# The last step of an inverse transform as three products over 128 rows, in place of four over 96

## The chip, the cores and the metric

One core of one Trainium2 chip. The metric is the device time of one execution, in microseconds.

## The reference

In short (the whole has intermediate names):

```python
def _attn_ref(x, filt_r, filt_i):           # x: 8 batches x 3008 tokens x 256 channels
    X = np.fft.rfft(x, axis=1)
    Y = X * (filt_r + 1j * filt_i)[None]
    return np.fft.irfft(Y, n=x.shape[1], axis=1).astype(np.float32)

def _moe_ref(x, w_gate, w_val, w_out):      # x: 24064 x 256, d_ff 1536
    g = x @ w_gate
    return (g / (1 + np.exp(-g)) * (x @ w_val) @ w_out).astype(np.float32)
```

Everything is fp32. Most of the time goes to the second part. The kernel does the transforms of batch b+1 between the products of batch b.

## The kernel before

A transform of 3008 = 47 x 64 tokens is done in steps. The change concerns the last step of the inverse one, `stage3`, and what feeds it. An intermediate `d2` in DRAM holds 48 rows (24 frequencies, real and imaginary) for each of 64 residues n2 and 256 channels. `load_t4` brings one piece of it, `stage3` multiplies by a table over the 96 rows (two halves h of 48), and ACT (ScalarE) and DVE (VectorE) evacuate the result, that is, bring it from PSUM to `y`. PE in the profile's lines is TensorE.

```python
def load_t4(self, k, i, part=None):
    # ... (the first chunk of batch 0 has a path of its own)
    t = t4pool.tile([NK, NH, C], FP32, ...)              # NK = 96, NH = 4, C = 256
    self.load(out=t, in_=self.d2_rows[:, ts(2 * k + i, NH), :])

def stage3(self, k, step):                               # step 0..3, k = chunk 0..3
    i, cb = divmod(step, 2)
    ps = ...                                             # one PSUM bank
    psv = ps...[:, 0:TH].rearrange("p (n r) -> p n r", n=NH)   # TH = 4 x 94 = 376
    for n in range(NH):
        pin(nc.tensor.matmul(out=psv[:, n, :], lhsT=self.t4[k, i][:, n, ts(cb, 128)],
                             rhs=wi_t, start=n == 0, stop=True, skip_group_check=True))
    yield
    # ... evacuations to y
```

In this text a block is one `stage3` step, with four products before and three after. A weight load brings `lhsT` into TensorE's array ahead of the matmul that uses it. A record is one entry of the profile's list of instructions. `pd` is the PSUM tile that a block writes, `wa`, `wk`, `we`, `wA`, `wF` and `wG` are tiles of the second part. Column 2 n1 + h of each 94 belongs to half h. So 94 columns of a product hold two interleaved sets of 47, each of which uses 48 of the 96 rows; the other half of the table is zeros. That is the waste that the change goes after.

Of the kernel before, what the change touches and what calls it, by code (L numbers as in the profile page):

```python
# [41 lines left out]
FP32 = mybir.dt.float32  # L42
U32 = mybir.dt.uint32
# [5 lines left out]
B, S, C = 8, 3008, 256  # L49
# [4 lines left out]
N1, N2 = 47, 64  # L54
NS, NQ = 24, 64
NR = 2 * N1
NK = 4 * NS

NH = 4
# [4 lines left out]
NT = 3  # L64
NG = 3
# [4 lines left out]
NV = 2  # L70
# [39 lines left out]
PIECES = ((0, 7), (7, 14), (14, 20), (20, 26))  # L110


def dft_tables():
    n1, n2 = np.arange(N1), np.arange(N2)
    s, q = np.arange(NS), np.arange(NQ)
    ph = 2 * np.pi * (np.outer(n1, s) % N1) / N1
    w = np.stack([np.cos(ph), -np.sin(ph)], 1)
    wf = np.zeros((N1, 2, NS, 2, 2))
    wi = np.zeros((NS, 2, 2, N1, 2))

    v = np.stack([2 * np.cos(ph), -2 * np.sin(ph)], 0)
    v[0, :, 0], v[1, :, 0] = 1.0, 0.0
    for h in range(2):
        wf[:, h, :, :, h] = w.transpose(0, 2, 1)
        wi[:, :, h, :, h] = v.transpose(2, 0, 1) / S


    kap = np.where(q[:, None] < 32, s + N1 * q[:, None], s + N1 * (95 - q[:, None]))
    sg = np.where(q < 32, 1.0, -1.0)[:, None]
    th = 2 * np.pi * ((n2[:, None, None] * kap) % S) / S  # L130
    c, sn = np.cos(th), np.sin(th)
    d = np.zeros((2, N2, NS, 2, NQ))
    d[0, :, :, 0] = c.transpose(0, 2, 1)
    d[1, :, :, 0] = sn.transpose(0, 2, 1)
    d[0, :, :, 1] = (-sn * sg).transpose(0, 2, 1)
    d[1, :, :, 1] = (c * sg).transpose(0, 2, 1)
    d = d.reshape(128, NS, 128)
    de = np.stack([d, d.transpose(2, 1, 0)], 2)
    f32 = np.float32
    return (wf.reshape(NR, NK).astype(f32), wi.reshape(NK, NR).astype(f32),  # L140
            np.ascontiguousarray(de).astype(f32))


@with_exitstack
def kernel(
# [8 lines left out]
    out: bass.AP,  # L154
):
    nc = tc.nc
    wf_host, wi_host, de_host = dft_tables()
    wf_dram = nc.inline_tensor(wf_host, name="wf_tbl")
    wi_dram = nc.inline_tensor(wi_host, name="wi_tbl")
    de_dram = nc.inline_tensor(de_host, name="de_tbl").ap()  # L160
    unit_dram = nc.inline_tensor(np.eye(128, dtype=np.float32), name="unit_tbl")

    def pool(name, bufs, space=None):
# [6 lines left out]
    t4pool = pool("t4", 2)  # L170
# [35 lines left out]
    one = cpool.tile([128, 1], FP32)  # L206
# [15 lines left out]
    pin = tc.keep_in_program_order  # L222

    def add(eng, dst, a, b):
        return eng.tensor_tensor(out=dst, in0=a, in1=b, op=ALU.add)  # L225
# [224 lines left out]
    preparation = Preparation()  # L450
    TICKS = 20



    def bank(name):
# [11 lines left out]
    class Spectral:  # L467


        def __init__(self, b):  # L470
            self.b = b
            self.d1, self.d2 = [dram_tiles[2 * (b % 2) + i] for i in range(2)]
            self.d1_rows = self.d1.rearrange("a (h n) c -> (a h) n c", h=2)
            self.d2_rows = self.d2.rearrange("a (h n) c -> (a h) n c", h=2)
            self.x, self.t2, self.f, self.tb, self.p, self.t4, self.y = {}, {}, {}, {}, {}, {}, {}
            self.real = {}
# [27 lines left out]
        def load_two(self, u):  # L504
            if u < N_TWO:
                self.tb[u] = lend("tb", u).rearrange("p i (k c) -> p i k c", k=2)
                self.load(out=self.tb[u], in_=de_dram[:, ts(u, NV)])

                f = lend("f", u).rearrange("p (k i) c -> p k i c", k=2)
                self.f[u] = f  # L510
                for rows, view in filter_parts():
                    r, part = rows.start, rows.start // 64
                    for at in (r, r + 64) if part == 0 else (r,):
                        self.load(out=f[at:at + 32, part], in_=view(NV * u, NV))
                self.t2[u] = lend("t2", u)
                self.load(out=self.t2[u], in_=self.twos(self.d1, u))
# [10 lines left out]
        def load_t4(self, k, i, part=None):  # L527
            if part is not None:

                t = f0[0:NK, ts(i, NH), :]  # L530
                r = (slice(0, 64), slice(64, NK))[part]
                self.load(out=t[r], in_=self.d2_rows[r, ts(i, NH), :])
            else:
                t = t4pool.tile([NK, NH, C], FP32, name=f"t4_{self.b}_{k}_{i}", tag="t4")
                self.load(out=t, in_=self.d2_rows[:, ts(2 * k + i, NH), :])
            self.t4[k, i] = t

        def bank(self, name):
# [76 lines left out]
        def stage2b(self, u):  # L615

            pt, tb = self.p.pop(u), self.tb.pop(u)
            ps = self.bank(f"pc_{self.b}_{u}")
            for i in range(NV):
                pin(nc.tensor.matmul(out=ps[:, i, :], lhsT=tb[:, i, 1, :],  # L620
                                     rhs=pt[:, i, :], start=True, stop=True))
            g = self.place("g", u)
            yield
            if self.b == 0 and u == N_TWO - 1:
                for i in range(NV):
                    pin(nc.scalar.copy(out=g[:, i], in_=ps[:, i]))
            else:
                pin(nc.scalar.copy(out=g, in_=ps))
            queue = nc.scalar if self.b or u >= 8 else nc.sync
            pin(queue.dma_start(out=self.twos(self.d2, u), in_=g))  # L630

        def stage3(self, k, step):

            if step == 0:
                self.y[k] = ypool.tile([128, 8, TQ], FP32, name=f"y_{self.b}_{k}", tag="y")
            i, cb = divmod(step, 2)
            ps = (self.bank if k == 0 else fbank)(f"pd_{self.b}_{k}_{step}")
            psv = ps.rearrange("p a b -> p (a b)")[:, 0:TH].rearrange("p (n r) -> p n r", n=NH)
            for n in range(NH):
                pin(nc.tensor.matmul(out=psv[:, n, :],  # L640
                                             lhsT=self.t4[k, i][:, n, ts(cb, 128)],
                                             rhs=wi_t, start=n == 0, stop=True,
                                             skip_group_check=True))
            yield

            y = self.y[k]

            def tokens(part, parts):
                return y[:, part:part + parts].rearrange("p t (r n) -> p n (t r)", n=NH)

            if cb == 0:
                pin(nc.scalar.copy(out=tokens(2 * i, 2), in_=psv))
                return
            for t in range(2):
                a, c = 2 * i + t, psv[:, :, ts(t, N1)]
                b, v, k = tokens(a, 1), tokens(4 + a, 1), KS[a]
                if k == 0:
                    pin(nc.scalar.copy(out=v, in_=c))
                elif k == -1:
                    pin(add(nc.vector, v, c, b))  # L660
                else:
                    pin(nc.vector.scalar_tensor_tensor(
                        out=v, in0=b, scalar=-float(k), in1=c, op0=ALU.mult, op1=ALU.add))
# [164 lines left out]
    rpool = pool("raw", 1)  # L828
# [11 lines left out]
    with tc.tile_pool(name="start", bufs=1) as spool0:  # L840
# [12 lines left out]
        n = 0  # L853
# [34 lines left out]
        for u in range(N_TWO + lag):  # L888
            if u < N_TWO:
                spec.turn(u + 2)  # L890
                step = spec.stage2a(u)
# [26 lines left out]
        for p in ("A13", "A01"):  # L918
            at = SLOT[p]
# [62 lines left out]
    def chore(step, token, f, *args):  # L982
        chores.setdefault((step, token), []).append((f, args))

    chore(0, "B01", lambda: combine_sequence(cur.y[0], 3))
    for step in range(NT):
# [3 lines left out]
        if step < NCHUNK - 2:  # L990
            for i in range(2):
                chore(step, "A23", lambda k, i: cur.load_t4(k, i), step + 2, i)
    chore(NT, "W2", keep_y, NT)
    for step in range(NT - 1, NT * NG):
        chore(step, "A02" if step < NT else "P0", lambda s: reload_y(order_of(0)[s + 1][0], s), step)
    for step in range(NT, NT * NG):
# [5 lines left out]
    for b in range(B):  # L1002
        cur, nxt = spec, following if b + 1 < B else None
# [7 lines left out]
        one = [nxt.stage1(u) for u in range(N_ONE)] if nxt else []  # L1011
        two = []
# [23 lines left out]
        for step in range(NCHUNK * NG + (b == B - 1)):  # L1036
            ghost = step == NCHUNK * NG
            k, g = order_of(b)[min(step, NCHUNK * NG - 1)]
            this = None
            pieces = []  # L1040
            if not ghost:
                pieces = plan[step]
                this = Group(b, k, g, cur.y[k], sequence_of(cur, nxt, step))
                if b == 0:
                    preparation.finish(step)
                chunk = {0: 1, 2: 2, 5: 3}.get(step)
                if b and chunk:
                    for i in range(2):
                        cur.load_t4(chunk, i)
            elif before is None:  # L1050
                break
            ends = {ORDER[e - 1]: n for n, (_, e) in enumerate(PIECES)}
            last = ghost or b == B - 1 and step == NCHUNK * NG - 1
            for place, token in enumerate(SCHEDULE):
# [4 lines left out]
                op = token.rstrip("'")  # L1059
                if op[0] == "t":  # L1060
                    n = int(op[1])
                    ps = pieces_before if old else pieces
# [15 lines left out]
                if b + 2 < B and (step, op) == (9, "B01"):  # L1078
                    for u in range(2):
                        following.load_x(u)  # L1080
                if nxt and (step, op) == (10, "A12" if b else "E23"):
                    for i in range(2):
                        nxt.load_t4(0, i)
                for f, args in chores.get((step, op), ()) if b == 0 else ():
                    f(*args)
# [36 lines left out]
```

## Time and profile before

| | before |
|---|---|
| median, first three runs | 2950.47 us |
| TensorE busy | 99% |
| blocks in all: 8 batches x 16 | 128, of which 112 change |

The profile's view of one tile, pd, in the kernel before: records with duration min/median/max in ns.

```profile
L640 PE MATMUL pd<-wi_t,t x992: 246/275/421, 78.5 to 2817.6; 96*128 96x94 f32 x199
L652 ACT COPY y<-pd x62: 833/843/871, 79.6 to 2811.9; 128x376 f32<-128x376 f32 x62
```

The first line counts eight records for a block of four products; the second is the evacuation that mustn't get dearer.

### The profile page before, as it was taken

The numbers are of one execution on the slowest core, as the hardware profiler recorded it, in microseconds if no ns is written. First come the engines' busy times: TensorE is split into PE (matmuls) and PEld (weight loads), VectorE is DVE, ScalarE is ACT, GpSimd is POOL, SyncE is SP. The second block draws the span as 40 slices with busy tenths as digits, with TensorE's granted clock in tenths as the row PEclk, the third lists the DMA queues.
The fourth block names the chain that finished last, engine by engine and source line by source line (L and its number), as shares of the span: only waits on it lengthen the run. The fifth ranks groups of instructions, "written<-read, shape, count | busy, mean of one in ns | idle before, by whom it ended". The sixth has DMA issues, their size and how long they took to land.

```text
span 2946.9 us, 57623 instructions
## 1 busy us (share of the span) xinstructions
PE 2911.7 (99%) x20264; PEld 2816.1 (96%) x20264; DVE 1929.3 (65%) x4384; ACT 1609.9 (55%) x4208; POOL 1579.8 (54%) x1759
## 2 busy tenths in 40 slices
PE   7999999999999999999999999999999999999999
PEld 5889999999999999999999999999999999999999
DVE  6888765576655676557765667656666566766666
ACT  6775455545555555555455554555555555555554
POOL 3876655556444655455554456454564545555453
PEclk9999999999999999999999999999999999999999
DMA  8677855575555655556646566556665565644442
GB/s 232 212 255 245 299 188 184 174 229 180 178 179 185 222 186 171 182 188 200 213 152 194 188 195 212 162 176 203 194 199 171 177 211 190 201 138 152 148 129 88
DMA packets 217452, 558.57 MB, mean 190 GB/s; under 512 B 29962, under 2 KB 107642, under 8 KB 217166
## 3 DMA queue, kind: packets, MB, share of 16 engines
q1 hardware_dynamic: 171326, 485.59, 51.5%
q10 hardware_dynamic: 36912, 45.43, 4.6%
q0 software_dynamic: 8928, 23.89, 2.3%
q8 instruction: 162, 2.65, 0.4%
q14 instruction: 124, 1.02, 0.1%
HBM read 459.73 MB, written 95.05 MB: 188 GB/s over the span
## 4 chain that ended last, share of the span: by engine, by line
PE 94%; DVE 1%; POOL 1%; DMA 1%; issue 0%; ACT 0%; SPq 0%; DVEq 0%; POOLq 0%
PE wa L732 24%; PE wA L811 17%; PE wk L732 16%; PE we L732 12%; PE wG L811 9%; PE wF L811 4%; PE pd L640 4%; PE pa L548 3%; PE pc L620 2%; PE pb L588 2%; DMA y_t<-yt 0%; POOL y_t L225 0%; DVE h L779 0%; POOL wt_t L225 0%; POOL wt_t L228 0%
## 5 line engine op out<-in xcount | busy, mean ns | idle before, releaser
L732 PE MATMUL wa<-y_t,wt_t 128*128 128x188 f32 x4464 | 880.2, 323 | 5.2 <-issue 1.4
L732 PEld LDWEIGHTS wa<-y_t,wt_t 128*128 128x128 f32 x4464 | 730.0, 190 | 30.1 <-issue 17.3
L225 POOL TENSOR_TENSOR h<-h 128x376 f32<-128x376 f32 x190 | 183.1, 985 | 787.1 <-DVE h L779 777.5
L811 PE MATMUL wA<-wo_t,h 128*128 128x128 f32 x4608 | 577.7, 275 | 2.5 <-DVE o L225 2.0
L811 PEld LDWEIGHTS wA<-wo_t,h 128*128 128x128 f32 x4608 | 562.9, 192 | 16.2 <-issue 10.4
L732 PE MATMUL wk<-y,wt_t 128*128 128x188 f32 x2976 | 567.9, 324 | 0.0
L228 POOL TENSOR_TENSOR h<-h 128x376 f32<-128x376 f32 x570 | 553.5, 993 | 0.5
L732 PEld LDWEIGHTS wk<-y,wt_t 128*128 128x128 f32 x2976 | 479.2, 191 | 25.9 <-issue 19.8
L228 DVE TENSOR_TENSOR we<-we,m 128x376 f32<-128x376 f32 x576 | 318.6, 556 | 196.9 <-PE we L732 138.4
L732 PE MATMUL we<-y_t,wt_t 128*128 128x188 f32 x2232 | 431.5, 323 | 1.4 <-ACT we L763 1.4
L732 PEld LDWEIGHTS we<-y_t,wt_t 128*128 128x128 f32 x2232 | 369.4, 190 | 1.8 <-ACT we L763 1.7
L228 POOL TENSOR_TENSOR D<-f,f 128x376 f32<-128x376 f32 x288 | 281.0, 989 | 104.6 <-ACT f L747 103.9
L232 DVE SCALAR_TENSOR_TENSOR y<-wk,c 128x376 f32<-128x376 f32 x480 | 245.1, 543 | 133.8 <-ACT we L763 83.2
L767 ACT COPY m<-wa 128x376 f32<-128x376 f32 x576 | 272.0, 472 | 88.2 <-PE wa L732 87.0
L774 ACT ACTIVATE g<-wa 128x188 f32<-128x188 f32 x576 | 188.1, 327 | 190.6 <-PE wa L732 182.6
L811 PE MATMUL wG<-wo_t,h 128*128 128x128 f32 x2304 | 288.3, 275 | 0.6 <-DVE o L225 0.6
L811 PEld LDWEIGHTS wG<-wo_t,h 128*128 128x128 f32 x2304 | 281.4, 192 | 0.8 <-DVE o L225 0.8
L774 ACT ACTIVATE u<-we 128x188 f32<-128x188 f32 x576 | 189.0, 328 | 168.8 <-DVE we L228 149.9
L747 ACT ACTIVATE f<-wk 128x376 f32<-128x376 f32 x288 | 139.3, 484 | 235.4 <-PE wk L732 214.3
L751 ACT COPY c<-wk 128x376 f32<-128x376 f32 x288 | 136.0, 472 | 226.0 <-PE wk L732 226.0
L754 DVE SCALAR_TENSOR_TENSOR x<-wk,f 128x376 f32<-128x376 f32 x192 | 104.6, 545 | 235.8 <-PE wk L732 230.0
L763 ACT COPY we<-y 128x376 f32<-128x376 f32 x480 | 224.1, 487 | 33.7 <-DVE h L779 14.7
(142 smaller groups left out, 3915.9 us busy)
## 6 DMA issues: line engine op xcount, KB each, us to landing
wt_t<-w_all SPq DMA_DIRECT2D x174, 896.0 KB
wt_t<-w_all SPq DMA_DIRECT2D x174, 768.0 KB
t<-d SPq DMA_DIRECT2D x62, 384.0 KB
d<-t ACTq DMA_DIRECT2D x112, 192.0 KB
lent<-de_tbl SPq DMA_DIRECT2D x84, 256.0 KB
lent<-in_filt_r_dram SPq DMA_DIRECT2D x336, 64.0 KB
lent<-d SPq DMA_DIRECT2D x84, 256.0 KB
d<-lent ACTq DMA_DIRECT2D x84, 256.0 KB
```

The source lines that it names most:

```text
L225: return eng.tensor_tensor(out=dst, in0=a, in1=b, op=ALU.add)
L228: return eng.tensor_tensor(out=dst, in0=a, in1=b, op=ALU.subtract)
L232: return nc.vector.scalar_tensor_tensor(out=dst, in0=a, scalar=-1.0, in1=b, op0=ALU.mult, op1=ALU.subtract)
L640: pin(nc.tensor.matmul(out=psv[:, n, :], lhsT=self.t4[k, i][:, n, ts(cb, 128)], rhs=wi_t, start=n == 0, stop=True, skip_group_check=True))
L732: pin(nc.tensor.matmul(out=ps[:, z], lhsT=self.wt[:, SLOT[p], z], rhs=rhs, start=start and z == 0, stop=True, skip_group_check=True))
L747: pin(act.mul(self.small(f"f{i}", f"f{i}", 1), t[f"k{i}"], -1.0))
L751: pin(act.copy(out=self.small(f"c{i}", f"c{i}", 1), in_=t[f"k{i}"]))
L754: pin(v.scalar_tensor_tensor(out=dst, in0=t[f"k{j}"], scalar=-1.0, in1=t[f"f{i}" if j == 3 else f"D{at}"], op0=ALU.mult, op1=ALU.add))
L763: pin(act.copy(out=self.bank(f"e{at}"), in_=t[f"y{at}"]))
L767: pin(act.copy(out=self.small(f"m{at}", "m", 4), in_=t[f"a{at}"]))
L774: pin(act.activation(out=self.small(op, "g", 3, 1)[:, 0], in_=ps[:, 1], func=AF.Silu))
L811: pin(nc.tensor.matmul(out=self.tiles[at][:, t, :], lhsT=self.hs[i][:, HID[p], t0:t0 + 128], rhs=wo_t[:, JB * q + i, WO[p], :], start=star ...
```

## The change

From batch 1 on, `d2` is kept by tokens with real and imaginary rows side by side. A group (n2, h) is then 48 adjoining rows, eight groups are 384 rows, and these fill three tiles of 128 rows without zeros. A group that lies across a tile's edge occurs in two products, so the products have 3, 4 and 3 groups of 47 columns: 141, 188 and 141.

```diff
+BACK = (((0, 0, 0, 48), (1, 48, 0, 48), (2, 96, 0, 32)),
+        ((4, 64, 0, 48), (5, 112, 0, 16), (2, 0, 32, 16), (3, 16, 0, 48)),
+        ((5, 0, 16, 32), (6, 32, 0, 48), (7, 80, 0, 48)))
 ... (tables: back from BACK; later = de with its columns in the new order)
-                self.load(out=self.tb[u], in_=de_dram[:, ts(u, NV)])
+                self.load(out=self.tb[u], in_=later_dram[:, ts(u, NV)])
 ... load_t4, from batch 1 on:
+                    rows = self.d2_tokens.rearrange("(h n) a c -> h (n a) c", h=2)
+                    rows = rows[:, ts(at, 2 * NS * NH)]
+                    for j in range(2):
+                        self.load(out=t[64 * j:64 * j + 64, 1],
+                                  in_=rows[j, 128 * (1 - j):128 * (1 - j) + 64])
+                        self.load(out=t[:, 2 * j], in_=rows[j, 64 * j:64 * j + 128])
 ... the store of d2, from batch 1 on:
+            rows = self.d2_tokens.rearrange("n (p s) c -> (n p) (s c)", p=2)
+            pin(queue.dma_start(out=rows[:, ts(u, NV * C)], in_=g.rearrange("q s c -> q (s c)")))
 ... stage3:
+            for j in range(len(BACK) if back else 0):
+                first = BACK_AT[j]
+                cols = back_t[0][:, first:first + N1 * len(BACK[j])]
+                if j == 1:
+                    rows = flat[:, 1:2 * 187 + 1].rearrange("p (z y) -> p z y", z=2)[:, :, ::2]
+                else:
+                    at = j // 2 * (2 * N1 + 1)
+                    rows = flat[:, at:at + 6 * N1 - 1:2]
+                pin(nc.tensor.matmul(out=rows, lhsT=self.t4[k, i][:, j, ts(cb, 128)], rhs=cols,
+                                     start=j == 0, stop=True, skip_group_check=True))
-            for n in range(NH):
+            for n in range(0 if back else NH):
 ... the second load of a chunk is issued later in its step; the table back is loaded once in batch 0
```

The order of columns in the bank is kept, so that evacuations stay as they are. Each product therefore writes every second element of the bank.

More of the change, by code (lines that the diff above doesn't have):

```diff
@@ L110 @@
 PIECES = ((0, 7), (7, 14), (14, 20), (20, 26))
+BACK = (((0, 0, 0, 48), (1, 48, 0, 48), (2, 96, 0, 32)),
+        ((4, 64, 0, 48), (5, 112, 0, 16), (2, 0, 32, 16), (3, 16, 0, 48)),
+        ((5, 0, 16, 32), (6, 32, 0, 48), (7, 80, 0, 48)))
+BACK_AT = (0, 3 * N1, 7 * N1)
 def dft_tables():
@@ L125, in dft_tables @@
         wi[:, :, h, :, h] = v.transpose(2, 0, 1) / S
+    one = wi[:, :, 0, :, 0].transpose(1, 0, 2).reshape(2 * NS, N1)
+    back = np.zeros((128, 10 * N1))
+    for tile_, first in zip(BACK, BACK_AT):
+        for i, (_, row, a, rows) in enumerate(tile_):
+            back[row:row + rows, first + N1 * i:first + N1 * (i + 1)] = one[a:a + rows]
     kap = np.where(q[:, None] < 32, s + N1 * q[:, None], s + N1 * (95 - q[:, None]))
@@ L138, in dft_tables @@
     de = np.stack([d, d.transpose(2, 1, 0)], 2)
+    pairs = np.arange(128).reshape(2, N2).T.ravel()
+    later = np.stack([de[:, :, 0], de[:, :, 1][:, :, pairs]], 2)
     f32 = np.float32
     return (wf.reshape(NR, NK).astype(f32), wi.reshape(NK, NR).astype(f32),
-            np.ascontiguousarray(de).astype(f32))
+            back.astype(f32), np.ascontiguousarray(de).astype(f32),
+            np.ascontiguousarray(later).astype(f32))
 @with_exitstack
@@ L156 @@
     nc = tc.nc
-    wf_host, wi_host, de_host = dft_tables()
+    wf_host, wi_host, back_host, de_host, later_host = dft_tables()
     wf_dram = nc.inline_tensor(wf_host, name="wf_tbl")
     wi_dram = nc.inline_tensor(wi_host, name="wi_tbl")
+    back_dram = nc.inline_tensor(back_host, name="back_tbl")
     de_dram = nc.inline_tensor(de_host, name="de_tbl").ap()
+    later_dram = nc.inline_tensor(later_host, name="later_tbl").ap()
     unit_dram = nc.inline_tensor(np.eye(128, dtype=np.float32), name="unit_tbl")
@@ L451, with load_back @@
     TICKS = 20
+    back_t = []
+    def load_back():
+        t = rpool.tile([128, 2, 128, 2], U32, name="back", tag="raw", bufs=2)
+        t = t.bitcast(FP32).rearrange("p b f two -> p (b f two)")
+        back_t.append(t[:, 0:10 * N1])
+        pin(nc.sync.dma_start(out=back_t[0], in_=back_dram.ap()))
     def bank(name):
@@ L473, in __init__ @@
             self.d1_rows = self.d1.rearrange("a (h n) c -> (a h) n c", h=2)
+            self.d2_tokens = self.d2.rearrange("a n c -> (a n) c").rearrange(
+                "(n a) c -> n a c", n=N2)
             self.d2_rows = self.d2.rearrange("a (h n) c -> (a h) n c", h=2)
@@ L533, in load_t4 @@
             else:
-                t = t4pool.tile([NK, NH, C], FP32, name=f"t4_{self.b}_{k}_{i}", tag="t4")
-                self.load(out=t, in_=self.d2_rows[:, ts(2 * k + i, NH), :])
+                t = t4pool.tile([128, NH, C], FP32, name=f"t4_{self.b}_{k}_{i}", tag="t4")
+                at = 2 * k + i
+                if self.b == 0:
+                    self.load(out=t[0:NK], in_=self.d2_rows[:, ts(at, NH), :])
+                else:
[5 more added lines that the diff above has]
+                        self.load(out=t[:, 2 * j], in_=rows[j, 64 * j:64 * j + 128])
             self.t4[k, i] = t
@@ L629, in stage2b @@
             queue = nc.scalar if self.b or u >= 8 else nc.sync
-            pin(queue.dma_start(out=self.twos(self.d2, u), in_=g))
+            if self.b == 0:
+                pin(queue.dma_start(out=self.twos(self.d2, u), in_=g))
+                return
+            rows = self.d2_tokens.rearrange("n (p s) c -> (n p) (s c)", p=2)
+            pin(queue.dma_start(out=rows[:, ts(u, NV * C)], in_=g.rearrange("q s c -> q (s c)")))
         def stage3(self, k, step):
@@ L638, in stage3 @@
             psv = ps.rearrange("p a b -> p (a b)")[:, 0:TH].rearrange("p (n r) -> p n r", n=NH)
-            for n in range(NH):
+            flat = ps.rearrange("p a b -> p (a b)")
+            back = self.b
+            for j in range(len(BACK) if back else 0):
[3 more added lines that the diff above has]
+                    rows = flat[:, 1:2 * 187 + 1].rearrange("p (z y) -> p z y", z=2)[:, :, ::2]
+                else:
+                    at = j // 2 * (2 * N1 + 1)
[3 more added lines that the diff above has]
+            for n in range(0 if back else NH):
                 pin(nc.tensor.matmul(out=psv[:, n, :],
-                                             lhsT=self.t4[k, i][:, n, ts(cb, 128)],
+                                             lhsT=self.t4[k, i][0:NK, n, ts(cb, 128)],
                                              rhs=wi_t, start=n == 0, stop=True,
@@ L993 @@
     chore(NT, "W2", keep_y, NT)
+    chore(NT * NG - 1, "P0", load_back)
     for step in range(NT - 1, NT * NG):
@@ L1047 @@
                 if b and chunk:
-                    for i in range(2):
-                        cur.load_t4(chunk, i)
+                    cur.load_t4(chunk, 0)
             elif before is None:
@@ L1080 @@
                         following.load_x(u)
-                if nxt and (step, op) == (10, "A12" if b else "E23"):
-                    for i in range(2):
+                if b and chunk and op == "B01":
+                    cur.load_t4(chunk, 1)
+                for i in range(2):
+                    if nxt and (step, op) == (10, ("A12", "E23")[i] if b else "E23"):
                         nxt.load_t4(0, i)
```

## The prediction

> **What bounds the kernel now.** I read first the page's shares and slices, then the chain that ended last, then TensorE's groups by shape, then TensorE's order of time in one stretch of a middle batch, and last the load queue's order of time in the same stretch.
>
> The page's first part and its slices:
> ```profile
> span 2946.9 us, 57623 instructions
> PE 2911.7 (99%) x20264; PEld 2816.1 (96%) x20264; DVE 1929.3 (65%) x4384; ACT 1609.9 (55%) x4208; POOL 1579.8 (54%) x1759
> PE   7999999999999999999999999999999999999999
> PEclk9999999999999999999999999999999999999999
> DMA  8677855575555655556646566556665565644442
> ```
> TensorE is busy from the second slice to the last at full clock. The other engines have a third or more of the span free and the DMA engines about two fifths. The page's chain says the same by line:
> ```profile
> PE 94%; DVE 1%; POOL 1%; DMA 1%; issue 0%; ACT 0%; SPq 0%; DVEq 0%; POOLq 0%
> PE wa L732 24%; PE wA L811 17%; PE wk L732 16%; PE we L732 12%; PE wG L811 9%; PE wF L811 4%; PE pd L640 4%; PE pa L548 3%; PE pc L620 2%; PE pb L588 2%; DMA y_t<-yt 0%; POOL y_t L225 0%; DVE h L779 0%; POOL wt_t L225 0%; POOL wt_t L228 0%
> ```
> So the end is set by the sum of TensorE's work, and what the change touches (tile pd, line 640) is 4% of it, some 105 to 130 us. TensorE's groups by shape (columns: line, engine, operation, out<-in, partitions x columns, count, then busy us and mean ns, then idle before):
> ```profile
> L732 PE MATMUL wa<-y_t,wt_t 128*128 128x188 f32 x4464 | 880.2, 323 | 5.2 <-issue 1.4 <-DMA y_t<-yt 1.3 <-ACT m L767 1.2
> L640 PE MATMUL pd<-wi_t,t 96*128 96x94 f32 x992 | 128.3, 272 | 0.0
> ```
> The pd products never waited for anything: idle 0.0. Their mean of 272 ns is a latency of overlapping instructions and not their price. The price is read from where one run of matmuls starts and the next starts. TensorE's order of time (start us, us, what):
> ```profile
> 1501.25 1.47 PE L732 MATMUL wk<-y,wt_t 128*128 128x188 f32 x8
> 1502.56 1.50 PE L811 MATMUL wA<-wo_t,h 128*128 128x128 f32 x12
> 1503.89 1.44 PE L732 MATMUL wk<-y,wt_t 128*128 128x188 f32 x8
> 1505.17 0.80 PE L732 MATMUL wa<-y_t,wt_t 128*128 128x188 f32 x4
> 1505.81 0.80 PE L732 MATMUL wk<-y,wt_t 128*128 128x188 f32 x4
> 1506.44 1.03 PE L640 MATMUL pd<-wi_t,t 96*128 96x94 f32 x8
> 1507.31 1.53 PE L811 MATMUL wA<-wo_t,h 128*128 128x128 f32 x12
> 1508.67 0.80 PE L732 MATMUL wk<-y,wt_t 128*128 128x188 f32 x4
> ```
> Each fp32 product of the program shows as two matmul records and two weight loads (8 records for a block of 4 products). A record with 188 columns takes (1505.81 - 1505.17)/4 = 160 ns, one with 128 columns (1503.89 - 1502.56)/12 = 111 ns, and one of pd with 94 columns (1507.31 - 1506.44)/8 = 109 ns. The last two are the point: 94 columns cost as much as 128. The pd products stand on a floor, and it isn't the streaming of columns.
>
> **What the Trainium skill says, and whether this trace agrees.** First, "TensorE: Matmul & The Clock Gate", section "LDWEIGHTS (loading the stationary operand)": a weight load takes the number of its columns divided by 1.2, in ns, whatever the contraction. For 128 columns that is 107 ns, and section "Back-to-back issue gap" gives a warm gap of N/2.4 + 2.5 ns. If each of the two records streams its columns at two cycles each (my reading), that is 2N/2.4 + 2.5: 159.2 ns for 188 (the trace has 160), 109 for 128 (111), 81 for 94. The trace has 109, so there the weight load binds. The page and the trace agree.
>
> Second, "PSUM — Partial Sum Buffer", section "Specifications (TRN2)": lines of 8 bytes, and "any non-contiguous AP slows matmuls significantly". The new products write every second fp32 element, one per 8-byte line. Every matmul of the kernel before writes adjoining columns, so its trace neither supports nor denies this. It is the main doubt.
>
> Third, "DMA: Bandwidth & Descriptors", section "Rules for kernel authors", on two transfers to disjoint partition halves: "Don't bother", as they share the same engines. The change splits one third of each load that way, so I expect no speed from it, only one more issue.
>
> **The change part by part.** The blocks: 8 batches x 4 chunks x 4 steps = 128 of 4 products, so 1024 records, which are the 992 above and 32 with another source tile. Batch 0 keeps its form, so 112 blocks change.
>
> Removed: 112 blocks of 8 records. The block above takes 870 ns; others of the same stretch took 860 (1500.39 to 1501.25), 870 and 860, so I use 865: 112 x 0.865 = 96.9 us.
>
> Added: 112 blocks of 3 products over 128 rows with 3, 4 and 3 groups of 47 columns, which is 141, 188 and 141. By the formula that the 188-column records confirm, a record of 141 columns takes 282/2.4 + 2.5 = 120 ns (an estimate from that page's section and this trace), just above the weight-load floor, and one of 188 takes 160. A block is 2 x (120 + 160 + 120) = 800 ns, and 112 x 0.800 = 89.6 us. The streamed columns rise from 376 to 470 a product set, but two of eight weight loads go. That is why the gain is so much less than the quarter that "three for four" suggests: 65 ns of 865, or 7.5%.
>
> The sum on TensorE: 96.9 - 89.6 = 7.3 us, 0.25% of the time. As TensorE is the bound and never waits, all of it should reach the end.
>
> Moved off the path: the evacuations to y (ACT and DVE) read the same PSUM layout, so they keep their durations. The store of d2 takes rows of 2 KB in place of 1 KB. A load of t4 takes four transfers with 384 rows of 1 KB in place of one with 96 rows of 4 KB; the bytes are the same. The issue records of SP show about 0.4 us for such a transfer, so a step with a chunk (two loads, one step of about 30 us in three) gets 6 x 0.4 = 2.4 us more on a queue that mostly waits for weight buffers. The load queue's order of time:
> ```profile
> 1487.86 0.80 SPq L479 DMA_DIRECT2D t<-d  x2
> 1488.76 38.34 SPq L376 DMA_DIRECT2D wt_t<-w_all  x7
> ```
> The two loads are issued by 1488.7, and the first block that reads them starts at 1500.39, 11.7 us later. The change also issues the second half of a chunk later in the step. By the program's schedule this one goes from 58% of a step to 82% of it, and its block comes at 47% of the next: 0.65 x 30 = 19 us. So there is room. The table is loaded once, in batch 0, into a buffer that the weights' preparation has left. The new transform table has the size of the old one. I count all of this as nothing.
>
> **The rivals.** (1) Strided PSUM writes slow the products, as the skill's PSUM page warns. If every column then takes twice as long, a block is 2 x (240 + 320 + 240) = 1600 ns and the kernel gains 112 x 0.735 = 82 us: 3033, slower by 2.8%. If they cost a quarter more, a block is 1000 ns and the kernel is 15 us slower. The break-even is 8% on the new block. Against it: an fp32 column takes two array cycles here where the formula without the factor has one, so an output every 0.83 ns instead of every 0.42 may leave time for a line each. Also, the author kept this order, and evacuations, when a contiguous order was to be had. I give any clear slowdown one chance in five, and the full doubling one in ten.
>
> (2) The loads come late. Four transfers for one, behind a wait on the last store of d2, in a queue that also carries the weights (the slices give the DMA engines 0.5 to 0.6): pd would wait at its first product of a half, or a weight reload would land late. For it: the queue is served in order, and a wait in it holds everything behind. Against it: 12 us of room and TensorE's idle before pd of 0.0. If 2 us were lost at each of 28 chunks it would be 56 us, but I expect fewer than 5 us in total.
>
> (3) The saving is taken back by another engine, as TensorE gets to its next wait sooner. DVE at 65% and ACT at 55% over a step of 30 us say no; the saving is 0.26 us in a step with four blocks.
>
> **Range and chances.** 2950.5 - 7.3 = 2943.2 us, rounded to 2943. Without any penalty I expect 2938 to 2948, allowing for the 4 us by which the three runs of before differ. The upper end is stretched to 2953 for a small penalty of the strided writes or a few late loads. Faster by over 2% (below 2891) would need 59 us of the 96.9 that the blocks cost in all: 1%. Slower by over 2% (above 3009) needs nearly the doubling of rival 1 or waits in most steps: 10%. Within 2%: 89%.
>
> **What would show it right or wrong.** In the changed trace: pd has 32 + 96 or so records of the old form and 672 of the new (112 x 6). From a pd block's start to the next run is about 800 ns, with 120 ns for records of 141 columns and 160 for 188; clearly more, with no idle before it, would be the strided write. Idle before pd stays near 0; a wait there for a DMA t<-d would be rival 2. Idle before wa or wk for wt_t would be a late weight reload. The evacuations of pd by ACT stay as long. The prediction is wrong if a block of six takes over 865 ns, or if TensorE's idle time grows by over 7 us.

## The result, and the profile after

| | before | after |
|---|---|---|
| first timing (4 runs each, medians) | 2950.61 us | 2937.79 us |
| ratio, 95% interval | | 0.9958 (0.9941 to 0.9975) |
| second timing (9 and 5 runs, medians) | 2953.43 us | 2938.78 us |
| ratio, 95% interval | | 0.9951 (0.9937 to 0.9965) |

The result is correct, 0.4 to 0.5% faster. That is some 12 to 15 us where 7.3 were predicted. The first median, 2937.79 us, lies 0.2 us below the lower end of the predicted range (2938), the second, 2938.78, just inside it.

The page of the changed kernel:

```profile
span 2935.5 us, 57365 instructions
PE 2901.7 (99%) x20040; PEld 2805.6 (96%) x20040; DVE 1927.4 (66%) x4384; ACT 1609.7 (55%) x4208; POOL 1579.9 (54%) x1759
```

TensorE has 224 matmuls and 224 weight loads fewer (112 blocks x 2), and is still the bound at 99%. The other engines' busy times are the same within 2 us. TensorE's groups of the new products, by shape:

```profile
L696 PE MATMUL pd<-back,t 128*128 128x141 f32 x448 | 90.4, 283 | 0.0
L696 PE MATMUL pd<-back,t 128*128 128x188 f32 x224 | 54.1, 322 | 0.0
```

There are 672 records of the new form, and no idle time before them. The evacuation by ACT takes as long as before (a median of 840 ns, where it was 843):

```profile
L711 ACT COPY y<-pd x62: 835/840/888, 80.1 to 2800.7; 128x376 f32<-128x376 f32 x62
```

The same stretch in TensorE's order of time, changed kernel (a merged line shows one of its shapes; the six records of a block are two each of 141, 188 and 141 columns):

```profile
1500.97 0.96 PE L696 MATMUL pd<-back,t 128*128 128x141 f32 x6
1501.77 1.50 PE L870 MATMUL wA<-wo_t,h 128*128 128x128 f32 x12
1503.11 0.80 PE L791 MATMUL wk<-y,wt_t 128*128 128x188 f32 x4
```

From the block to its follower, the run of matmuls right behind it in TensorE's order of time: 0.80 us, where it was 0.87. But look at the follower, too. These twelve wA records take 1503.11 - 1501.77 = 1.34 us. In the lines that the prediction shows of before, the twelve wA records behind the block take 1508.67 - 1507.31 = 1.36, and those not behind one 1503.89 - 1502.56 = 1.33. The same with wk: eight records behind a block took 1502.56 - 1501.25 = 1.31, eight others 1505.17 - 1503.89 = 1.28. So before, the run behind a block paid some 0.03 us of the block's price. The starts of single records in the trace, over 112 blocks, in ns (the intervals are medians, the block is a mean):

| | intervals from the block's first record | block, from its start to its follower's | first interval of a 188-column follower |
|---|---|---|---|
| before | 85, 109, 112, 112, 112, 112, 112, 112 | 864 | 190 |
| after | 120, 120, 163, 158, 123, 119 | 804 | 158 |

The first interval of a run of 188 columns elsewhere is 159 ns, so the whole price before is 864 + 190 - 159 = 895 ns, which is within 1 ns of 8 x 112. After it is 804. The Trainium skill, "Perfetto Trace Analysis", section "Tensor Engine Instruction (MATMUL, LD_WEIGHTS)", says that a matmul's reported start is the start of its data prefetch, ahead of its work in the array. The trace is in keeping with that: the second record of a 94-column block starts 85 ns after the first, near the 81 ns that the prediction estimates for streaming, and only from the third on are the starts 109 to 112 ns apart. So each delay shows one record late, and the block's last one shows in its follower. This reading is argued from the page; the sum of starts is measured.

The load queue's order of time in the changed kernel:

```profile
1482.36 2.74 SPq L511 DMA_DIRECT2D t<-d  x4
1485.20 1.85 SPq L396 DMA_DIRECT2D wt_t<-w_all  x2
1487.10 2.21 SPq L511 DMA_DIRECT2D t<-d  x4
```

Each half of a chunk (i = 0 or 1) is now four transfers, issued within 2.2 to 2.7 us. The block that reads the first half starts at 1495.01, 10 us after its last issue, and the block that reads the second at 1507.00, 18 us after. The loads aren't on the path.

### The profile page after: what moved, and what is told of

The parts are those of the page before. It is cut to its first block, busy times and chain, and to the rows that moved or that the text cites. A ratio compares the mean times of both kernels' runs of the same rounds, so it can differ in the third digit from the quotient of the medians.

```text
span 2935.5 us, 57365 instructions
## 1 busy us (share of the span) xinstructions
PE 2901.7 (99%) x20040; PEld 2805.6 (96%) x20040; DVE 1927.4 (66%) x4384; ACT 1609.7 (55%) x4208; POOL 1579.9 (54%) x1759
## 4 chain that ended last, share of the span: by engine, by line
PE 94%; DVE 1%; POOL 1%; ACT 0%; issue 0%; DVEq 0%; POOLq 0%
PE wa L791 24%; PE wA L870 17%; PE wk L791 16%; PE we L791 12%; PE wG L870 9%; PE wF L870 4%; PE pa L590 3%; PE pd L696 3%; PE pc L662 2%; PE pb L630 2%; PE pd L699 0%; POOL y_t L245 0%; DVE h L838 0%; POOL wt_t L245 0%; POOL wt_t L248 0%
## 5 line engine op out<-in xcount | busy, mean ns | idle before, releaser
L826 ACT COPY m<-wa 128x376 f32<-128x376 f32 x576 | 272.0, 472 | 87.1 <-PE wa L791 85.9
```

What stands on the lines that cost most here:

```text
L826: pin(act.copy(out=self.small(f"m{at}", "m", 4), in_=t[f"a{at}"]))
```

## The experiments

The first theory after the trace, called the floor theory below: what a record of N columns costs is the slower of its weight load (112 ns) and its streaming (the prediction's estimate, 2N/2.4 + 2.5 ns), block by block with the follower's share; the loads, the rows and the stride of the writes cost nothing. Rivals: the transfers bring a part of the gain; the 32 ns of the follower come from the change of 96 to 128 rows; the strided writes cost something.

One measure is far sharper than the time of a run. From the start of the first changed block (after some 420 us) to the start of the last matmul, traces of one kernel agree within 0.02 us. All traces, in us:

| kernel | first matmul to first changed block | from there to last matmul | ratio of times |
|---|---|---|---|
| before | 418.8 | 2521.24 | |
| before_twin | 418.9 | 2521.24 | 0.9996 |
| after | 417.9 | 2510.81 | 0.9958 |
| after_again | 420.1 | 2510.81 | 0.9951 |
| adjoining | 418.6 | 2510.81 | 0.9952 |
| products_only | 419.8 | 2511.22 | 0.9963 |
| products_twin | 418.1 | 2511.22 | 0.9960 |
| transfers_only | 424.3 | 2521.24 | 0.9990 |
| transfers_twin | 425.3 | 2521.23 | 1.0005 |
| four_on_128_rows | 420.1 | 2521.07 | 0.9987 |
| four_of_128_columns | 417.5 | 2521.25 | 0.9985 |
| six_halves | 420.8 | 2571.10 | 1.0157 |

**after_again**: the changed kernel, no edit, timed in five rounds.

> The changed kernel as it is, timed in more rounds. Floor theory: a record of 94 columns costs the pace of its weight load, 112 ns, in all eight records of a block; the block's own span of 864 ns in the trace before hides 32 ns that its follower pays (190 ns in place of 159). So 112 blocks cost 112 x 8 x 0.112 = 100.4 us before and 112 x 0.804 = 90.0 us now: 10.4 us less, 2940 against 2950.6. Rival (the transfers or something else bring a part): more than that, 12 to 13 us less, as the four runs so far gave.

2938.78 us against 2953.43, more than the floor theory's 10.4 us, as the rival expected. Behind the first changed block the trace shows 2521.24 - 2510.81 = 10.43 us, which is 112 x 93 ns, and no more. So the rest, if it is one, lies in the first 420 us.

**transfers_only**: the new layout, stores, loads and table, with the four products of before.

```diff
-            for j in range(len(BACK) if back else 0):
+            for j in range(0):
-            for n in range(0 if back else NH):
+            for n in range(NH):
-                 lhsT=self.t4[k, i][0:NK, n, ts(cb, 128)],
+                 lhsT=self.t4[k, i][0:NK, n % 3 if back else n, ts(cb, 128)],
```

> The new layout of d2, its stores, its loads and the new table, but the four products of before over 96 rows and 94 columns (the result is wrong on purpose). Floor theory: no gain, within 2 us of the kernel before; blocks of 864 ns with a follower at 190 ns. Rival (transfers bring a part): 2 to 6 us faster than before. Late loads would make it slower.

Ratio 0.9990 (0.9978 to 1.0003). The block is back to 0.87 us and its wA follower to 1.37:

```profile
1511.93 1.03 PE L699 MATMUL pd<-wi_t,t 96*128 96x94 f32 x8
1512.80 1.53 PE L870 MATMUL wA<-wo_t,h 128*128 128x128 f32 x12
1514.17 0.80 PE L791 MATMUL wk<-y,wt_t 128*128 128x188 f32 x4
```

Behind the first changed block not a hundredth of the gain is left: 2521.24. The timing alone would have left 3 us open: by the medians, 2948.29 against 2953.43 us, this kernel was 5 us faster, outside the 2 us of the floor theory and in the rival's range. The twins at the end of this section take that up.

**products_only**: the transfers and their places of before, and the three wide products over the 96 rows that those bring.

```diff
 ... (load_t4: the load of 96 rows, always)
-                if self.b == 0:
+                if True:
 ... (the store of before always; the table de; both loads of a chunk where they were)
-                pin(nc.tensor.matmul(out=rows, lhsT=self.t4[k, i][:, j, ts(cb, 128)], rhs=cols,
+                pin(nc.tensor.matmul(out=rows, lhsT=self.t4[k, i][0:NK, j, ts(cb, 128)], rhs=cols[0:NK],
```

> The stores, loads and their times of before, and three products of 141, 188 and 141 columns over the 96 rows that those loads bring (wrong on purpose). Floor theory: the whole gain, 10 us less than before; block 804 ns, the follower at 159 ns. Transfers theory: 6 to 8 us less only. If 96 rows in place of 128 were what makes the follower pay 32 ns, the follower would stay at 190 ns and the gain be 7 us.

Ratio 0.9963 (0.9951 to 0.9976), and 10.0 us less behind the first changed block. The follower takes 1.33 us again, and the first interval of a 188-column follower is 162 ns:

```profile
1503.04 0.97 PE L696 MATMUL pd<-back,t 96*128 96x141 f32 x6
1503.85 1.50 PE L870 MATMUL wA<-wo_t,h 128*128 128x128 f32 x12
1505.18 0.80 PE L791 MATMUL wk<-y,wt_t 128*128 128x188 f32 x4
```

So the products bring the gain, and the follower's 32 ns don't come from the rows. With 96 rows and the transfers of before it takes 0.4 us more than the changed kernel (2511.22 against 2510.81); which of the two does that isn't shown.

**adjoining**: the changed kernel with products that write adjoining columns.

```diff
-                if j == 1:
-                    rows = flat[:, 1:2 * 187 + 1].rearrange("p (z y) -> p z y", z=2)[:, :, ::2]
-                else:
-                    at = j // 2 * (2 * N1 + 1)
-                    rows = flat[:, at:at + 6 * N1 - 1:2]
+                at = (0, 3 * N1, 5 * N1)[j]
+                rows = flat[:, at:at + N1 * len(BACK[j])]
```

> The changed kernel, but each product writes adjoining columns of the bank in place of every second (wrong on purpose). If strided writes are free, the same time within 1 us and block 804 ns. If they cost what the block has over the formula (804 against 798 ns), the block falls to 798 ns and the kernel by 0.6 us. If they cost much, the block falls to where 141 columns are bound by the weight load at 112 ns (about 770).

Ratio 0.9952, block 803.7 ns in the mean where the changed kernel has 803.7, and 2510.81 us behind the first changed block, the same to the hundredth:

```profile
1501.66 0.97 PE L693 MATMUL pd<-back,t 128*128 128x141 f32 x6
1502.47 1.50 PE L867 MATMUL wA<-wo_t,h 128*128 128x128 f32 x12
1503.80 0.80 PE L788 MATMUL wk<-y,wt_t 128*128 128x188 f32 x4
```

Writing every second element cost these fp32 products nothing. The 6 ns that the block has over the formula (804 against 798) stay without a cause: they aren't the stride.

**four_on_128_rows**: transfers_only with the table's 128 rows in the four products (`lhsT` all 128 rows, `rhs=back_t[0][:, 0:NR]`, 94 columns).

> The new transfers and four products of 94 columns, but over all 128 rows (wrong on purpose). Floor theory: the rows do not matter, so as before: block 864 ns, follower 190 ns, time of the kernel before within 2 us. Rival (the follower's 32 ns come from going over from 96 to 128 rows): follower 159 ns, 3.5 us faster than before.

Block 863 ns, first interval of the follower 190 ns, 2521.07 us behind the first changed block: as before.

```profile
1507.64 1.03 PE L699 MATMUL pd<-back,t 128*128 128x94 f32 x8
1508.50 1.53 PE L875 MATMUL wA<-wo_t,h 128*128 128x128 f32 x12
1509.87 0.80 PE L796 MATMUL wk<-y,wt_t 128*128 128x188 f32 x4
```

With products_only this settles the rows from both sides. The ratio, 0.9987 (0.9973 to 1.0), again looked like a small gain, and the medians, 2949.69 against 2952.33 us, differ by more than the 2 us expected.

**four_of_128_columns**: transfers_only with 36% more columns.

```diff
 ... (the loop over j is off, as in transfers_only)
+            for n in range(NH if back else 0):
+                pin(nc.tensor.matmul(out=flat[:, 83 * n:83 * n + 128],
+                                     lhsT=self.t4[k, i][0:NK, n % 3, ts(cb, 128)],
+                                     rhs=back_t[0][0:NK, 0:128], start=n == 0, stop=True,
+                                     skip_group_check=True))
```

> The new transfers and four products over 96 rows, but of 128 columns in place of 94, overlapping in the bank (wrong on purpose). Floor theory: 36% more columns for nothing, as 109 ns of streaming still lie under the 112 ns of the weight load: 8 x 112 = 892 to 896 ns to the next run, the follower back at 159 ns, time as before within 2 us. If the columns were the price (the reading in which 94 columns cost less than 112 ns), 892 - 864 = 28 ns a block more, 3 us slower.

```profile
1505.13 1.05 PE L699 MATMUL pd<-back,t 96*128 96x128 f32 x8
1506.02 1.50 PE L875 MATMUL wA<-wo_t,h 128*128 128x128 f32 x12
1507.36 0.80 PE L796 MATMUL wk<-y,wt_t 128*128 128x188 f32 x4
```

The block takes 0.89 us to its follower, which then pays 1.34 as any other run. From the block's start to the end of the follower it is 2.23 us, and 2.23 in the lines of before: 34 columns more a record for nothing. What moved is only where the price shows, 893 ns and a first interval of 163 in place of 864 and 190. Behind the first changed block: 2521.25 us against 2521.24. The times missed what was expected: 2948.47 against 2952.33 us, ratio 0.9985 (0.9972 to 0.9997), a gain clear of one by its interval though the trace has none.

**six_halves**: the changed kernel with each product cut in two by columns, the result right.

```diff
-                pin(nc.tensor.matmul(out=rows, lhsT=self.t4[k, i][:, j, ts(cb, 128)], rhs=cols,
-                                     start=j == 0, stop=True, skip_group_check=True))
+                half = N1 * (len(BACK[j]) // 2)
+                if j == 1:
+                    parts = [(rows[:, z], cols[:, half * z:half * z + half]) for z in range(2)]
+                else:
+                    parts = [(rows[:, 0:half], cols[:, 0:half]), (rows[:, half:], cols[:, half:])]
+                for z, (to, by) in enumerate(parts):
+                    pin(nc.tensor.matmul(out=to, lhsT=self.t4[k, i][:, j, ts(cb, 128)], rhs=by,
+                                         start=j + z == 0, stop=True, skip_group_check=True))
```

> The changed kernel with each of its three products cut in two by columns: six products of 70, 71 or 94 columns, the same columns and rows in all, the right result. Floor theory: 12 records at 112 ns are 1344 ns in place of 804, 540 ns more in 112 blocks: 60 us slower than the changed kernel, 50 us (1.7%) slower than before. If columns were the price: within 5 us of the changed kernel.

The cut fell at whole groups, so the parts have 47 and 94 columns, not the 70 and 71 that the expectation names. 2997.79 us, ratio 1.0157 (1.0144 to 1.017), and 60.3 us more than the changed kernel behind the first changed block, where 60 were expected:

```profile
1530.21 1.47 PE L702 MATMUL pd<-back,t 128*128 128x47 f32 x12
1531.52 1.53 PE L876 MATMUL wA<-wo_t,h 128*128 128x128 f32 x12
```

Twelve records take 1309 ns (median) to their follower and 31 ns in it: 1340 of the 1344 expected. With the same columns and rows, only the number of records went up, each with its weight load.

**The three twins.** Three kernels with the old price of a block had come out at 0.9985 to 0.9990, and products_only with the full gain of the products at 0.9963, against 0.9951 to 0.9958. That looks like some 3 us from the transfers, while the traces behind the first changed block deny it. The trace of transfers_only showed another place to look. The profile's table by stretches, 60 to 90 us, with the granted clock behind the engines' columns, first the kernel before, then transfers_only:

```profile
60.00:90.00 30.00, 25.36 (x134) 18.82 (x133) 23.56 (x50) 21.07 (x51) 21.57 (x29) 1.00 0.71 219
```

```profile
60.00:90.00 30.00, 26.91 (x98) 19.45 (x97) 18.55 (x39) 16.61 (x37) 16.04 (x24) 0.74 0.51 146
```

In that run TensorE was granted 0.74 of its clock in this stretch and did 98 matmuls in place of 134; from 72.2 to 85.9 us the clock was 0.50, where the kernel before had 1.00. At its 341st matmul it was 7.8 us behind the kernel before (4.0 at the 300th, which the next expectation names by mistake), some 340 us ahead of the first changed block, where 5.5 us were left. This is called a late start below. So three kernels were timed again, without an edit: before against itself, the products alone and the transfers alone.

> The kernel before against itself, a control. Start theory: the runs of every kernel fall in two groups some 6 us apart, set in the first 90 us, ahead of any changed instruction (the trace of transfers_only is 7.8 us late at its 300th matmul already), so the two sides differ only by how many of their runs started late: the ratio lies within 0.999 and 1.001, quick starts at 2947 to 2951 us. If the order of the runs favoured the second kernel, 0.9985 to 0.999, as three kernels with old products and new transfers showed.

> The products alone again. Start theory: quick starts at 2937 to 2941 us as the changed kernel's, late ones at 2944 to 2946. Transfers theory (they bring 3 us of the gain): also the quick starts some 3 us above those of the changed kernel.

> The transfers alone again. Start theory: quick starts at 2947 to 2951 us like those of before, late ones at 2953 to 2956, after the first changed block as before to 0.2 us. Transfers theory: quick starts 3 us below those of before.

The control: 0.9996 (0.9983 to 1.0008). The products alone: 0.9960 (0.9948 to 0.9972), 2937.39 to 2938.71 us in five runs, among the changed kernel's times. The transfers alone: 1.0005 (0.9993 to 1.0018), so the 3 us are gone; three of its six runs lay at 2954 to 2955 us and the others at 2947 to 2950. Its trace fell on a late start again, with 0.74 granted from 60 to 90 us, and is as before to 0.01 us behind the first changed block. So what the first timings showed beyond 10.4 us was, in the main, the share of late starts among the runs. They were seen by trace in transfers_only and transfers_twin alone; for the kernel before they are inferred. The mean clock supports it: of the 21 runs of the kernel before that the experiments were timed against, the 13 up to 2951.2 us have 0.998 or 0.999, and seven of the eight above have 0.996 or 0.997. Runs at 0.998 or more average 2949.5 us for the kernel before (14 runs) and 2938.3 us for after, after_again and adjoining (12 runs), 11.2 us apart. The sign isn't perfect: a run of four_on_128_rows at 2948.9 us has 0.997. Why the clock stays low for longer in some runs isn't settled.

## Why the prediction was right or wrong

- **TensorE sets the end and all that it saves arrives.** Right: blocks and followers together saved 112 x 92 ns = 10.3 us by their starts, and 10.43 us were gone from the first changed block to the last matmul.
- **The floor: 94 columns cost as much as 128.** Right, and shown by four_of_128_columns and six_halves: the records of short products come at 112 ns each on average. That this floor is the weight load, as the prediction says, is argued and not shown: in all these runs a record has a load of 128 columns of its own, so none of them separates the load from another fixed cost of a record.
- **A block before costs 865 ns, 96.9 us in all.** This term was mis-sized. It is 8 x 112 = 896 ns, 100.3 us. The prediction measured from the block's start to its follower's start, and the follower held 32 ns of it. The two wk runs of eight in its own lines, 1.31 and 1.28 us, showed it and weren't compared. Its own test, a block of over 865 ns, couldn't find this error.
- **A block after costs 800 ns, 89.6 us in all.** Right: 804 ns, 90.0 us.
- **The sum, 7.3 us.** 10.4 by the two terms as measured. The remaining 2 to 4 us of the first two timings are, as the twins and the clocks indicate, starts that fell differently; the products alone repeated gave 0.9960, some 12 us, with the same 10.0 in the trace. That the result stayed about the lower end of the range is luck: the range was drawn from the scatter of three runs, and not from a doubt about the price of a block.
- **Rival 1, strided writes.** It had one chance in five and fell: adjoining equals the changed kernel.
- **Rival 2, late loads.** It fell: no idle time before pd in the trace, 10 us of room in the stretch shown, and transfers_only as before. The issue of a transfer took 0.55 to 0.7 us in place of the 0.4 assumed, which cost nothing.
- **Rival 3, another engine.** It fell: TensorE's waits are no longer than before.

No version that beats both came out of this. The 141-column records are 8 ns above the floor, and the 384 rows of eight groups already fill three tiles of 128, so no further product can go this way. The 16 blocks of batch 0 keep the old form; at 93 ns each they are worth 1.5 us at most, which wasn't tried.

## What to carry to other kernels

Where TensorE is the bound, count products with their weight loads as well as columns: here an fp32 product's record cost 112 ns at 94 and at 128 columns alike and some 120 ns at 141, and fewer, wider products were worth it even though they streamed more columns. Read the price of a group of matmuls from its start to the end of the run behind it, compared with the same run elsewhere, as part of the price can show there: 32 ns of 895 here. And for an effect below the scatter of the times, compare two traces from a fixed instruction to another: here that agreed to 0.02 us where whole runs scattered by 8.

## What the Trainium skill lacked or had wrong

- "PSUM — Partial Sum Buffer", section "Specifications (TRN2)", says that any non-contiguous access pattern slows matmuls significantly. For the fp32 products of this case, which write every second element, it doesn't: 803.7 ns a block with and without the stride, 2510.81 us behind the first changed block in both.
- "TensorE: Matmul & The Clock Gate", section "LDWEIGHTS (loading the stationary operand)", gives a weight load as the number of its columns over 1.2, which is 107 ns for 128. In runs of short fp32 products each record took 112 ns, at 94 columns as at 128 (and 1309 + 31 ns for twelve records of 47 and 94). If the load sets this pace, as is argued here, the page is 5% low.
- No page says that part of the price of a run of short matmuls can show in the run behind it: 32 ns after records of 94 columns, 4 ns after those of 128.
